# Nystrom attention and two MLPs on one core: another order of steps for the second MLP's weight sums, y loaded a group earlier, and low halves moved to GpSimd

## The chip, the core and the metric

The kernel runs on one core of a Trainium2 chip. The metric is the device time of one execution in microseconds (us). The engines are named as in the profile: PE (TensorE, matrix products), DVE (VectorE), ACT (ScalarE), POOL (GpSimd) and SP (the queue that issues the transfers). Each engine runs its own instructions in the order in which they were written, and waits on semaphores for the others.

## The reference, cut

```python
def _attn_ref(q, k, v):                # 4 batches, 8 heads, 576 x 64, 32 landmarks
    A, Bm, C = sm(q, k_lm), sm(q_lm, k_lm), sm(q_lm, k)      # softmaxes
    Z = Bm.T / (norm1(Bm) * norminf(Bm) + 1e-06)
    for _ in range(6):
        Z = 2 * Z - Z @ Bm @ Z
    return A @ Z @ C @ v
def _moe_ref(x, w_in, w_out):          # 2304 tokens, 512 -> 2048 -> 512
    h = x @ w_in
    return (h - np.tanh(h)) @ w_out
def _moe2_ref(x, w_in, w_out):         # the same sizes
    h = x @ w_in
    return (h * np.tanh(softplus(h))) @ w_out
```

The result is `_moe2_ref` of `_moe_ref` of the attention. Inputs and outputs are float32.

## The kernel before

**Splitting.** A float32 factor is kept as two parts: a high half, which ACT makes by a copy to fp32r, and a low half, the difference that DVE or POOL makes with a `tensor_tensor`. A product is then three matmuls: high by high, high by low, low by high.

**First MLP.** It runs in 128 slots (NS = 128), one for 288 tokens and 128 of the 2048 hidden columns. Slot `s` issues `h1(s)` (6 matmuls, L635 to L637), `y1(s - 3)` in two halves (12 matmuls, L708, L709, L712) and `vec(s)`, which makes the activation on ACT and DVE: `mk` (L665), `g = h * e` (L671), `th` (L672), then for the slot before `g = q * g` (L682) and `copy_predicated` (L686), and for the slot before that the split of `g` into `gg` (L99 on ACT, L100 for the low half). `E()` chooses the engine of `mk` and of the low half: POOL in slots 24 to 103, DVE elsewhere. Up to slot 115 a scheduler may move instructions; from slot 116 on the order is as written.

**Second MLP.** The 2304 tokens are cut into 3 units of 768 (u = 0, 1, 2), the hidden columns into 8 parts (j). That makes 24 groups, k = 8u + j. A group multiplies 2 by 2 blocks by Strassen's scheme in Winograd's form, with 7 products p = 0 to 6 (`product`, L783 to L785, 6 matmuls each) and sums of blocks on either side. Between the products stand the units of the last group's second matrix (`o2_units`, L841 to L843); in group 0 there are the last halves of `y1` in their place. `combine(k, p)` takes a product out of PSUM (L806 on DVE), and `mish` makes the activation (L796 and L797 on ACT, L799 on DVE). Two PSUM buffers hold the products, so product p + 2 can only begin when `combine` of p has read its buffer.

**The weights' sums.** While unit 0 runs, `w2_cycles` decodes the second MLP's weights and makes the sums `X` (L185) and their halves `W2c[j][q]` (tiles P: high L178, low L182), and stores them; later units load them again. One cycle has 7 steps, one to a product: cycle j + 1 runs beside group j. The order in which the products need the halves is given by

```python
WI = ((1, 2), (1, 1), (0, 1), (0, 3), (0, 2), (1, 0), (0, 0))
```

so product 0 reads `W[1][2]` and product 1 reads `W[1][1]`, which is written with `W[1][0]` by the pair of instructions of shape 128x2x256 (128x512 in the profile).

**The y sums.** `y_prep(u)` loads four blocks of y for a unit, makes the sums `s1`, `s2`, `a21 - ...` (L742), and the halves `yk` (high L751, low L752) of seven operands; the tiles `AT` hold the seventh. `Y[u + 1, p]` lies in the buffer of `Y[u, p]`, so it can be written only between product p of the last group of a unit and product p of the next one. `part` and `parts` lay the generators' steps beside the products: one step of `y_prep` and one of `w2_cycles` at a product.

Of the kernel before, what the change touches and what calls it, by code (L numbers as in the profile page):

```python
# [8 lines left out]
F32 = mybir.dt.float32  # L9
# [20 lines left out]
def kernel(  # L30
# [19 lines left out]
    NS = 32 * B  # L50
# [91 lines left out]
    def w2_cycles():  # L142
        raws, halves = {}, {}

        def has(x, j):
            return 0 <= j < NJ

        def fetch(x, j):
            if has(x, j):
                raws[x, j] = load_raw(ONE[x](j))  # L150

        def cast(x, j):
            if has(x, j):
# [12 lines left out]

        def o_hi(x, j):
            if has(x, j):
                w = W2o[2 * j + (x == "d")] = wo_p.tile([128, 2, 512], F32R, tag="w", name="w")
                A.activation(out=w[:, 0, :], in_=o32[x, j], func=ACTF.Copy)  # L170

        def o_lo(x, j):
            if has(x, j):
                w = W2o[2 * j + (x == "d")]
                V.tensor_tensor(out=w[:, 1, :], in0=o32.pop((x, j)), in1=f32(w[:, 0, :]), op=ALU.subtract)

        def hi(W, i, src):
            A.activation(out=W[:, i:i + src.shape[1], 0, :], in_=src, func=ACTF.Copy)  # L178

        def lo(W, i, src):  # L180
            n = src.shape[1]
            V.tensor_tensor(out=W[:, i:i + n, 1, :], in0=src, in1=f32(W[:, i:i + n, 0, :]), op=ALU.subtract)  # L182

        def minus(o, x, y):
            V.tensor_tensor(out=o, in0=x, in1=y, op=ALU.subtract)  # L185

        def keep(j):
            for q in range(2):
                n = 4 - q
                nc.sync.dma_start(out=w2s[j][q][:, 0:n, :], in_=f32(W2c[j][q][:, 0:n].rearrange("p n t c -> p n (t c)")))  # L190

        fetch("a", 0)
        fetch("b", 0)
        for j in range(NJ + 1):
            i = j < NJ

            cast("a", j)
            if j:
                lo(W2c[j - 1][1], 0, rows[j - 1][:, 0:2])
                keep(j - 1)  # L200
                yield 0
            o_join("c", j - 1)
            yield 0
            cast("d", j - 1)
            yield 1

            if i:
                X = rows[j] = p2["X"].tile([128, 6, 256], F32, tag="X", name="X")
                joined("a", j, X[:, 0:4:3, :])
                yield 0  # L210
                cast("b", j)
            o_hi("c", j - 1)
            o_join("d", j - 1)
            yield 1

            fetch("c", j)
            if i:
                joined("b", j, X[:, 1:3, :])
                yield 0
            o_hi("d", j - 1)  # L220
            o_lo("c", j - 1)
            yield 1

            fetch("a", j + 1)
            if i:
                minus(X[:, 4:6, :], X[:, 1:3, :], X[:, 0:2, :])
                yield 0
            o_lo("d", j - 1)
            yield 1

            fetch("d", j)
            if i:
                W = W2c[j] = [P_p.tile([128, 4, 2, 256], F32R, tag="P", name="P") for q in range(2)]
                hi(W[1], 2, X[:, 0:1])
                hi(W[0], 0, X[:, 2:6])
                minus(X[:, 1], X[:, 2], X[:, 4])
            yield 1

            fetch("b", j + 1)
            if i:  # L240
                lo(W[1], 2, X[:, 0:1])
                yield 0
                minus(X[:, 0], X[:, 1], X[:, 3])
            yield 1

            cast("c", j)
            if i:
                hi(W[1], 0, X[:, 0:2])
                lo(W[0], 0, X[:, 2:6])
            yield 1  # L250

    def w2c_load(j):
        W = W2c[j] = [P_p.tile([128, 4, 2, 256], F32R, tag="P", name="P") for q in range(2)]
        for q in range(2):
            n = 4 - q
            nc.sync.dma_start(out=f32(W[q][:, 0:n].rearrange("p n t c -> p n (t c)")), in_=w2s[j][q][:, 0:n, :])
# [383 lines left out]
    def vec(s):  # L640
# [3 lines left out]
        if NW + 2 <= s < NS + 2:  # L644
            with tc.high_priority(20):
                g2 = sv[s - 2][0]
                gg = t1_p.tile([128, 2, HS], F32R, tag="gg", name="gg")
                split(g2, gg[:, 0, :], gg[:, 1, :], E())
                sv[s - 2] = gg
        if s == NS:  # L650
            A.preload_act_table_set("mish")
# [74 lines left out]
    def y_prep(u):  # L726

        def load(kh, th):
            t = raw_f32()[:, 0:2 * C2].rearrange("p (a n) -> p a n", a=2)
            n0 = 0  # L730
            while n0 < C2:
                i, o = divmod((2 * u + th) * C2 + n0, HS)
                n = min(C2 - n0, HS - o)
                nc.sync.dma_start(out=t[:, :, n0:n0 + n], in_=ys[i][:, 2 * kh:2 * kh + 2, o:o + n])
                n0 += n
            return t

        a21, a22, a11, a12 = load(0, 1), load(1, 1), load(0, 0), load(1, 0)
        s1, s2 = [p2["yf"].tile([128, 2, C2], F32, tag="yf", name="yf") for _ in range(2)]

        def tt(eng, o, x, y, op=ALU.subtract):
            (G if u == 0 else eng).tensor_tensor(out=o, in0=x, in1=y, op=op)  # L742

        def halves(p, t):
            if p < 6:
                y = p2["yk"].tile([128, 2, 2, C2], F32R, tag="yk", name="yk")
                y = Y[u, p] = [y[:, a] for a in range(2)]
            else:
                y = Y[u, p] = [AT_p.tile([128, 2, C2], F32R, tag="AT", name="AT") for a in range(2)]
            for a in range(2):  # L750
                A.activation(out=y[a][:, 0, :], in_=t[:, a], func=ACTF.Copy)  # L751
                V.tensor_tensor(out=y[a][:, 1, :], in0=t[:, a], in1=f32(y[a][:, 0, :]), op=ALU.subtract)  # L752
                yield 0

        yield 1
        tt(G, s1, a21, a22, ALU.add)
        yield 1
        tt(V, s2, s1, a11)
        yield from halves(0, a11)
        yield 1  # L760
        yield from halves(1, s2)
        tt(G, a21, a11, a21)
        yield 1
        yield from halves(2, a12)
        tt(V, s2, a12, s2)
        yield 1
        yield from halves(3, a21)
        yield 1
        yield from halves(4, s1)
        yield 1  # L770
        yield from halves(5, a22)
        yield 1
        yield from halves(6, s2)
        yield 1
# [110 lines left out]
    def group(k, bg2):  # L885
        if k:
            units = o2_units(k - 1)
        for p in range(7):
            product(k, p)
            if k:  # L890
                for _ in range(UNITS[p]):
                    next(units)
                gens = []
            else:
                cur[0] = NS + p // 2
                if p < 2 * LAG:
# [78 lines left out]
    if True:  # L975
# [44 lines left out]
            n += 1  # L1020
        gens = {}
        early = [NS - x for x in (14, 12, 10, 7, 5, 3, 1)]
        yearly = [NS - 26] + [NS - 24 + i + i // 3 for i in range(8)]

        def bg(s):
            b, i = s // 32, s % 32
# [38 lines left out]
        def bg2(k, p):  # L1065
# [58 lines left out]
```

## Time and profile before

| what | value |
|---|---|
| runs, median (lowest to highest) | 847.68 us (847.6 to 850.5), 3 runs |
| the profiled execution, its own time | 846.66 us |
| its span on the core | 844.9 us |
| around the span | 1.76 us |
| mean granted TensorE clock | 0.979 |
| PE busy | 797.4 us (94%) |
| DVE busy | 595.0 us (70%) |
| ACT busy | 510.1 us (60%) |
| POOL busy | 196.9 us (23%) |

The shares are means over stages with different limits. In a timeline a row's bracket is the time for which the engine stood idle before that row, and whose event ended it. The spans of DVE's instructions overlap by almost 0.1 us where one follows another, so their pace is read from start to start.

### The profile page before, as it was taken

What the parts mean: (1) busy time and instruction counts of PE and PEld (TensorE: products, weight loads), DVE (VectorE), ACT (ScalarE), POOL (GpSimd) and SP (SyncE); (2) the same over time, 40 slices, a digit from 0 to 9 for tenths busy, and PEclk for the clock granted to TensorE, in tenths of its full rate; (3) what the DMA queues carried; (4) which work ended last, traced back from release to release, by engine and by line L of the source; (5) the groups of instructions that cost most, each with busy time, mean ns of one, the idle gap of its engine ahead of it and who ended that gap; (6) DMA issues with size and microseconds to landing.
All of it is one profiled execution on the core that took longest, in us unless ns stands there. A gap on an engine that the chain in (4) does not pass through costs nothing. (4 is left out here: it accounts for less than half of the span.)

```text
span 844.9 us, 14775 instructions
## 1 busy us (share of the span) xinstructions
PE 797.4 (94%) x5384; PEld 673.9 (80%) x5384; DVE 595.0 (70%) x1315; ACT 510.1 (60%) x1213; POOL 196.9 (23%) x218
## 2 busy tenths in 40 slices
PE   4799999999999999989998999988999999999996
PEld 1446688789888998878987878877889898889885
DVE  7679999998799867899987777775434355333332
ACT  4586787888678867878885666555323235322322
POOL 0010007775688657770000000020000010000000
PEclk9599999999999999999999999999999999999998
DMA  9999231513034001301437557754523543522401
GB/s 319 323 339 352 108 133 50 184 51 108 35 123 162 1 31 51 123 31 50 130 138 264 187 224 251 259 188 161 199 88 100 181 144 124 209 91 91 172 1 74
DMA packets 41512, 123.62 MB, mean 146 GB/s; under 512 B 5856, under 2 KB 14560, under 8 KB 38368
## 3 DMA queue, kind: packets, MB, share of 16 engines
q1 hardware_dynamic: 40288, 118.49, 39.8%
q0 software_dynamic: 1152, 4.19, 1.2%
q8 instruction: 42, 0.69, 0.4%
q14 instruction: 30, 0.25, 0.1%
HBM read 94.36 MB, written 28.31 MB: 145 GB/s over the span
## 5 line engine op out<-in xcount | busy, mean ns | idle before, releaser
L796 ACT ACTIVATE gg<-x 128x384 fp32r<-128x384 f32 x72 | 37.8, 525 | 171.4 <-DVE x L806 170.9
L708 PE MATMUL y<-gg,w 128*128 128x288 f32 x448 | 134.0, 313 | 2.0 <-ACT gg L99 1.0
L709 PE MATMUL y<-gg,w 128*128 128x288 f32 x448 | 125.9, 296 | 0.0
L783 PE MATMUL h<-yk,P 128*128 128x384 f32 x288 | 99.0, 344 | 13.2 <-ACT P L178 5.9
L708 PEld LDWEIGHTS y<-gg,w 128*128 128x128 f32 x448 | 84.4, 188 | 21.9 <-issue 12.6
L712 PE MATMUL y<-gg,w 128*128 128x288 f32 x448 | 96.8, 298 | 3.3 <-POOL gg L100 2.4
L785 PE MATMUL h<-yk,P 128*128 128x384 f32 x288 | 98.1, 341 | 1.4 <-DVE P L182 0.7
L784 PE MATMUL h<-yk,P 128*128 128x384 f32 x288 | 97.1, 337 | 0.0
L100 POOL TENSOR_TENSOR gg<-g,gg 128x288 fp32r<-128x288 f32 x80 | 70.1, 876 | 112.9 <-ACT gg L99 110.6
L709 PEld LDWEIGHTS y<-gg,w 128*128 128x128 f32 x448 | 84.7, 189 | 1.1
L799 DVE TENSOR_TENSOR gg<-x,gg 128x384 fp32r<-128x384 f32 x72 | 40.2, 558 | 61.2 <-ACT x L797 61.2
L806 DVE TENSOR_TENSOR x<-x,h 128x384 f32<-128x384 f32 x72 | 39.8, 553 | 60.7 <-PE h L785 60.4
L665 POOL TENSOR_SCALAR mk<-s 128x288 uint8<-128x288 f32 x80 | 77.4, 968 | 10.7 <-ACT s L659 4.3
L686 DVE COPY_PREDICATED g<-mk,th 128x288 f32<-128x288 uint8 x128 | 75.6, 591 | 4.6
L843 PE MATMUL y<-w,gg 128*128 128x512 f32 x192 | 76.3, 398 | 0.0
L842 PE MATMUL y<-w,gg 128*128 128x512 f32 x192 | 76.3, 397 | 0.0
L712 PEld LDWEIGHTS y<-gg,w 128*128 128x128 f32 x448 | 71.5, 188 | 5.3 <-POOL gg L100 4.1
L841 PE MATMUL y<-w,gg 128*128 128x512 f32 x192 | 75.7, 394 | 0.0
L783 PEld LDWEIGHTS h<-yk,P 128*128 128x128 f32 x288 | 54.5, 189 | 25.4 <-ACT P L178 8.9
L742 POOL TENSOR_TENSOR yf<-raw 128x768 f32<-128x768 f32 x3 | 6.3, 2104 | 283.3 <-ACT x L797 168.2
L671 DVE TENSOR_TENSOR g<-h,s 128x288 f32<-128x288 f32 x128 | 56.8, 444 | 18.9 <-ACT th L660 18.4
L675 ACT ACTIVATE q<-q,bias_c 128x288 f32<-128x288 f32 x128 | 68.5, 535 | 2.4
(167 smaller groups left out, 1958.2 us busy)
## 6 DMA issues: line engine op xcount, KB each, us to landing
P<-w2s SPq DMA_DIRECT2D x16, 1024.0 KB, 4.9
w<-w1s SPq DMA_DIRECT2D x24, 512.0 KB, 4.5
P<-w2s SPq DMA_DIRECT2D x16, 768.0 KB, 5.6
w2s<-P SPq DMA_DIRECT2D x8, 1024.0 KB, 3.9
raw<-in_w1i_dram SPq DMA_DIRECT2D x16, 511.8 KB, 6.1
raw<-in_w1o_dram SPq DMA_DIRECT2D x16, 511.8 KB, 6.9
raw<-in_w2i_dram SPq DMA_DIRECT2D x16, 511.8 KB, 5.7
raw<-in_w2o_dram SPq DMA_DIRECT2D x16, 511.8 KB, 6.0
```

The source lines that it names most:

```text
L100: eng.tensor_tensor(out=L, in0=src, in1=f32(H), op=ALU.subtract)
L665: eng.tensor_scalar(out=mk, in0=e, scalar1=FT, scalar2=None, op0=ALU.is_ge)
L686: V.copy_predicated(out=g0, mask=mk0, data=t0)
L708: mm(yps[d], w[:, 0, c], gg[:, 0, :], start=(f == 0), stop=False)
L709: mm(yps[d], w[:, 1, c], gg[:, 0, :], start=False, stop=False)
L712: mm(yps[d], w[:, 0, c], gg[:, 1, :], start=False, stop=(f == NF - 1))
L783: mm(t, w[:, i, 0, c], y[a][:, 0], start=(a == 0), stop=False)
L784: mm(t, w[:, i, 0, c], y[a][:, 1], start=False, stop=False)
L785: mm(t, w[:, i, 1, c], y[a][:, 0], start=False, stop=(a == 1))
L841: mm(q, gg[:, 0, cs], w[:, 0, :], start=first, stop=False)
L842: mm(q, gg[:, 0, cs], w[:, 1, :], start=False, stop=False)
L843: mm(q, gg[:, 1, cs], w[:, 0, :], start=False, stop=last)
```

## The change

It has three parts.

- **Weights.** In `w2_cycles` the halves of `W[1][2]` are made at steps 3 and 4 (before: 5 and 6), the two subtractions that make `X[1]` and `X[0]` both at step 5 (before: 5 and 6), and the high half of `W[1][0:2]` at step 6 (before: 7). Its low half stays at step 1 of the next cycle. The low halves of the second matrix move from steps 3 and 4 to 4 and 6. The two tiles of a cycle are taken in the other order.
- **y.** For u = 1 and 2 the steps begin in the group next to last, at product 1 (before: product 6). The two blocks a21 and a22 are loaded into a pool `yl` of their own. The sums s1, s2 and a21 are made on POOL, and the low half of the second part of operands 1, 3 and 4 too. For u = 0 the steps stand at other slots, and the seventh operand's halves come in group 0.
- **First MLP.** From slot 107 on (NS - 21) the low half of `gg` is made on POOL (`late()`), 23 instructions; `mk` stays on DVE.

```diff
+    def late():
+        return G if 24 <= cur[0] < NS - 24 or cur[0] >= NS - 21 else V
...
             fetch("c", j)
             if i:
+                W = W2c[j] = w2c_tiles()
+                hi(W[1], 2, X[:, 0:1])
                 joined("b", j, X[:, 1:3, :])
-                yield 0
             o_hi("d", j - 1)
-            o_lo("c", j - 1)
             yield 1
...
                 minus(X[:, 4:6, :], X[:, 1:3, :], X[:, 0:2, :])
                 yield 0
-            o_lo("d", j - 1)
+                lo(W[1], 2, X[:, 0:1])
+            o_lo("c", j - 1)
             yield 1
...
-                hi(W[1], 2, X[:, 0:1])
                 hi(W[0], 0, X[:, 2:6])
                 minus(X[:, 1], X[:, 2], X[:, 4])
+                yield 0
+                minus(X[:, 0], X[:, 1], X[:, 3])
             yield 1
...
-                lo(W[1], 2, X[:, 0:1])
-                yield 0
-                minus(X[:, 0], X[:, 1], X[:, 3])
+                hi(W[1], 0, X[:, 0:2])
+            o_lo("d", j - 1)
             yield 1
...
-                hi(W[1], 0, X[:, 0:2])
                 lo(W[0], 0, X[:, 2:6])
...
-                split(g2, gg[:, 0, :], gg[:, 1, :], E())
+                split(g2, gg[:, 0, :], gg[:, 1, :], late())
...
+            t = p2["yl"].tile([128, 2, C2], F32, tag="yl", name="yl") if u and th else raw_f32()[
+                :, 0:2 * C2].rearrange("p (a n) -> p a n", a=2)
...
+                eng = G if u and a and p in (1, 3, 4) else V
+                tt(eng, y[a][:, 1, :], t[:, a], f32(y[a][:, 0, :]))
...
-        tt(V, s2, s1, a11)
+        tt(G, s2, s1, a11)
...
-        yearly = [NS - 26] + [NS - 24 + i + i // 3 for i in range(8)]
+        yearly = [NS - x for x in (26, 25, 24, 23, 22, 20, 18, 16, 14, 12, 9)]
...
-            if j == NJ - 2 and p == 6 and u + 1 < NU:
+            if j == NJ - 2 and p == 1 and u + 1 < NU:
                 gens["y"] = vec_only(y_prep(u + 1))
...
+            if j == NJ - 2 and p in (1, 2, 4, 5, 6) or j == NJ - 1 and p or j == 0 and p == 0:
                 mix.append(gens["y"])
```

**DVE at the end of a group of unit 0.** These rows stand in DVE's queue between the products 4 of one group and 1 of the next; X and P are the weights' sums and halves, w and y the second matrix, x, u and gg the group's own values. Before:

```order
L799 TENSOR_TENSOR gg<-x,gg 128x384
L806 TENSOR_TENSOR x<-x,h 128x384
L182 TENSOR_TENSOR P<-X,P 128x256
L799 TENSOR_TENSOR gg<-x,gg 128x384
L185 TENSOR_TENSOR X<-X 128x256
L806 TENSOR_TENSOR u_6630<-u_6630,h 128x384
L182 TENSOR_TENSOR P<-X,P 128x4x256
L799 TENSOR_TENSOR gg<-u_6630,gg 128x384
L182 TENSOR_TENSOR P<-X,P 128x2x256
```

After (line 809 is the old 799, 816 the old 806, 185 the old 182, 188 the old 185 and 178 the old 175):

```order
L809 TENSOR_TENSOR gg<-x,gg 128x384
L188 TENSOR_TENSOR X<-X 128x256
L816 TENSOR_TENSOR x<-x,h 128x384
L178 TENSOR_TENSOR w<-y,w 128x512
L809 TENSOR_TENSOR gg<-x,gg 128x384
L816 TENSOR_TENSOR u_6633<-u_6633,h 128x384
L185 TENSOR_TENSOR P<-X,P 128x4x256
L809 TENSOR_TENSOR gg<-u_6633,gg 128x384
L185 TENSOR_TENSOR P<-X,P 128x2x256
```

The subtraction that makes X[0] now stands two rows earlier, before the product's row, and a low half of the second matrix stands where the low half of W[1][2] stood. On ACT the high half that the last row reads stands ahead of the group's last `mish` instead of behind it.

**DVE in group 7, the last of unit 0.** yk, yf and AT belong to `y_prep(1)`. Before, from the joins of the second matrix on:

```order
L158 SCALAR_TENSOR_TENSOR y<-raw,top_127 128x512
L742 TENSOR_TENSOR yf<-yf,raw 128x768
L752 TENSOR_TENSOR yk<-raw,yk 128x384 x2
L806 TENSOR_TENSOR x<-x,h 128x384
L175 TENSOR_TENSOR w<-y,w 128x512
L752 TENSOR_TENSOR yk<-yf,yk 128x384
L799 TENSOR_TENSOR gg<-x,gg 128x384
L752 TENSOR_TENSOR yk<-yf,yk 128x384
L806 TENSOR_TENSOR x<-u_7399,h 128x384
```

After (line 161 is the old 158; 745 holds every sum and low half of `y_prep`):

```order
L161 SCALAR_TENSOR_TENSOR y<-raw,top_127 128x512
L745 TENSOR_TENSOR yk<-raw,yk 128x384 x2
L816 TENSOR_TENSOR x<-x,h 128x384
L809 TENSOR_TENSOR gg<-x,gg 128x384
L745 TENSOR_TENSOR yk<-yf,yk 128x384
L816 TENSOR_TENSOR x<-u_7404,h 128x384
```

The sum of 768 columns and one low half are gone from the rows, and a low half of the second matrix comes behind the product's row.

**POOL at its end.** Before, its queue closes with the sums of `y_prep`:

```order
L665 TENSOR_SCALAR mk<-s 128x288
L742 TENSOR_TENSOR yf<-raw,yf 128x768
L742 TENSOR_TENSOR yf<-raw 128x768
L742 TENSOR_TENSOR raw<-raw 128x768
L742 TENSOR_TENSOR yf<-raw 128x768
L742 TENSOR_TENSOR raw<-raw 128x768
```

After (103 is the old 100, 670 the old 665):

```order
L670 TENSOR_SCALAR mk<-s 128x288
L745 TENSOR_TENSOR yf<-raw,yf 128x768
L103 TENSOR_TENSOR gg<-g,gg 128x288 x23
L745 TENSOR_TENSOR yf<-yl 128x768
L745 TENSOR_TENSOR yf<-yf,raw 128x768
L745 TENSOR_TENSOR yl<-raw,yl 128x768
L745 TENSOR_TENSOR yk<-yf,yk 128x384
L745 TENSOR_TENSOR yk<-yl,yk 128x384
```

It gains the 23 low halves of `gg`, and for either later unit one sum and three low halves.

## Rows read from the trace of the kernel before

**Rows 1.** Windows: stretch, time, busy us of each engine, clock, DMA share, GB/s.
```profile
380.62:431.19 50.57, 49.11 (x358) 47.36 (x357) 49.25 (x136) 43.41 (x115) 1.04 (x1) 1.00 0.23 75
...
437.66:441.07 3.41, 3.41 (x15) 3.41 (x14) 2.36 (x5) 2.21 (x4) 0.00 (x0) 0.50 1.00 324
...
505.46:522.29 16.83, 16.18 (x78) 13.95 (x79) 12.89 (x24) 10.26 (x19) 0.00 (x0) 1.00 0.63 234
556.00:578.89 22.89, 17.25 (x79) 13.66 (x79) 16.26 (x27) 9.62 (x21) 2.63 (x1) 1.00 0.78 275
625.92:641.59 15.67, 15.67 (x80) 14.07 (x79) 5.93 (x11) 4.58 (x9) 0.00 (x0) 1.00 0.33 113
```
**Rows 2.** Timeline of PE: product 1's first matmul in groups 0, 1, 2, 8, 15, 16.
```profile
435.25 0.42 PE L783 MATMUL h<-yk,P 128*128 128x384 f32 x1 [1.17 <-DVE th L672]
...
453.40 0.44 PE L783 MATMUL h<-yk,P 128*128 128x384 f32 x1 [2.64 <-ACT P L178]
...
471.79 0.44 PE L783 MATMUL h<-yk,P 128*128 128x384 f32 x1 [0.54 <-ACT P L178]
...
578.89 0.41 PE L783 MATMUL h<-yk,P 128*128 128x384 f32 x1 [0.89 <-DVE u L806]
...
688.57 0.34 PE L783 MATMUL h<-yk,P 128*128 128x384 f32 x1
...
705.78 0.41 PE L783 MATMUL h<-yk,P 128*128 128x384 f32 x1 [0.89 <-DVE u L806]
```
**Rows 3.** Timeline of DVE at the end of group 4.
```profile
518.61 0.56 DVE L799 TENSOR_TENSOR gg<-x,gg 128x384 fp32r<-128x384 f32 x1 [0.81 <-ACT x L797]
...
521.12 0.56 DVE L799 TENSOR_TENSOR gg<-u,gg 128x384 fp32r<-128x384 f32 x1
...
522.27 0.69 DVE L182 TENSOR_TENSOR P<-X,P 128x512 fp32r<-128x512 f32 x1 [0.59 <-ACT P L178]
```
**Rows 4.** Timeline of ACT at the same place.
```profile
520.00 0.53 ACT L796 ACTIVATE gg<-u 128x384 fp32r<-128x384 f32 x1 [1.43 <-DVE u L806]
...
521.62 0.61 ACT L178 ACTIVATE P<-X 128x512 fp32r<-128x512 f32 x1
```
**Rows 5.** Timeline of DVE in slot 126, one round from L671 to L671.
```profile
428.39 0.44 DVE L671 TENSOR_TENSOR g<-h,s 128x288 f32<-128x288 f32 x1
...
429.12 0.45 DVE L100 TENSOR_TENSOR gg<-g,gg 128x288 fp32r<-128x288 f32 x1
429.48 0.45 DVE L682 TENSOR_TENSOR g<-q,g 128x288 f32<-128x288 f32 x1
...
430.45 0.44 DVE L671 TENSOR_TENSOR g<-h,s 128x288 f32<-128x288 f32 x1
```
**Rows 6.** Groups of DVE by line, slots 34 to 101, while POOL makes the low halves.
```profile
L686 DVE COPY_PREDICATED g<-mk,th 128x288 f32<-128x288 uint8 x68 | 42.9, 631 | 4.0
L682 DVE TENSOR_TENSOR g<-q,g 128x288 f32<-128x288 f32 x68 | 33.6, 494 | 1.4 <-ACT q L675 0.5
```
**Rows 7.** The same groups from 400 to 430 us, POOL idle.
```profile
L682 DVE TENSOR_TENSOR g<-q,g 128x288 f32<-128x288 f32 x13 | 5.8, 446 | 0.0
...
L686 DVE COPY_PREDICATED g<-mk,th 128x288 f32<-128x288 uint8 x12 | 5.8, 482 | 0.0
```
**Rows 8.** Timeline of DVE, product 2 of group 7.
```profile
560.77 0.96 DVE L742 TENSOR_TENSOR yf<-yf,raw 128x768 f32<-128x768 f32 x1 [1.84 <-DMA raw<-ys]
561.64 2.68 DVE L752 TENSOR_TENSOR yk<-raw,yk 128x384 fp32r<-128x384 f32 x2
```
**Rows 9.** Timeline of POOL, 545 to 570 us.
```profile
549.87 2.25 POOL L742 TENSOR_TENSOR yf<-raw 128x768 f32<-128x768 f32 x1 [168.20 <-ACT x L797]
...
560.80 2.63 POOL L742 TENSOR_TENSOR raw<-raw 128x768 f32<-128x768 f32 x1 [8.69 <-DMA raw<-ys]
```
**Rows 10.** Timeline of DVE in the group before, under POOL's first sum.
```profile
551.04 1.37 DVE L182 TENSOR_TENSOR P<-X,P 128x256 fp32r<-128x256 f32 x1
```
**Rows 11.** Groups of POOL by line, the whole span.
```profile
L100 POOL TENSOR_TENSOR gg<-g,gg 128x288 fp32r<-128x288 f32 x80 | 70.1, 876 | 112.9 <-ACT gg L99 110.6 <-POOL c L571 0.7
```

More of the change, by code (lines that the diff above doesn't have):

```diff
@@ L232, in w2_cycles @@
             if i:
-                W = W2c[j] = [P_p.tile([128, 4, 2, 256], F32R, tag="P", name="P") for q in range(2)]
-                hi(W[1], 2, X[:, 0:1])
                 hi(W[0], 0, X[:, 2:6])
                 minus(X[:, 1], X[:, 2], X[:, 4])
+                yield 0
+                minus(X[:, 0], X[:, 1], X[:, 3])
             yield 1
@@ L247, in w2_cycles, with w2c_tiles @@
             if i:
-                hi(W[1], 0, X[:, 0:2])
                 lo(W[0], 0, X[:, 2:6])
             yield 1
+    def w2c_tiles():
+        return [P_p.tile([128, 4, 2, 256], F32R, tag="P", name="P") for q in range(2)][::-1]
     def w2c_load(j):
-        W = W2c[j] = [P_p.tile([128, 4, 2, 256], F32R, tag="P", name="P") for q in range(2)]
+        W = W2c[j] = w2c_tiles()
         for q in range(2):
@@ L728, in load @@
         def load(kh, th):
-            t = raw_f32()[:, 0:2 * C2].rearrange("p (a n) -> p a n", a=2)
+            t = p2["yl"].tile([128, 2, C2], F32, tag="yl", name="yl") if u and th else raw_f32()[
+                :, 0:2 * C2].rearrange("p (a n) -> p a n", a=2)
             n0 = 0
@@ L736, in load @@
             return t
-        a21, a22, a11, a12 = load(0, 1), load(1, 1), load(0, 0), load(1, 0)
-        s1, s2 = [p2["yf"].tile([128, 2, C2], F32, tag="yf", name="yf") for _ in range(2)]
         def tt(eng, o, x, y, op=ALU.subtract):
-            (G if u == 0 else eng).tensor_tensor(out=o, in0=x, in1=y, op=op)
+            eng.tensor_tensor(out=o, in0=x, in1=y, op=op)
         def halves(p, t):
@@ L751, in halves @@
                 A.activation(out=y[a][:, 0, :], in_=t[:, a], func=ACTF.Copy)
-                V.tensor_tensor(out=y[a][:, 1, :], in0=t[:, a], in1=f32(y[a][:, 0, :]), op=ALU.subtract)
                 yield 0
+                eng = G if u and a and p in (1, 3, 4) else V
+                tt(eng, y[a][:, 1, :], t[:, a], f32(y[a][:, 0, :]))
+        a21, a22 = load(0, 1), load(1, 1)
+        s1, s2 = [p2["yf"].tile([128, 2, C2], F32, tag="yf", name="yf") for _ in range(2)]
+        yield 1
+        a11, a12 = load(0, 0), load(1, 0)
         yield 1
@@ L757, in y_prep @@
         yield 1
-        tt(V, s2, s1, a11)
+        tt(G, s2, s1, a11)
+        yield 1
+        tt(G, a21, a11, a21)
+        yield 1
         yield from halves(0, a11)
@@ L761, in y_prep @@
         yield from halves(1, s2)
-        tt(G, a21, a11, a21)
         yield 1
         yield from halves(2, a12)
-        tt(V, s2, a12, s2)
+        tt(V if u else G, s2, a12, s2)
         yield 1
@@ L901, in group @@
                     p2["g3"] = ctx.enter_context(tc.tile_pool(name="g3", bufs=3))
+                    p2["yl"] = ctx.enter_context(tc.tile_pool(name="yl", bufs=2))
             mix = bg2(k, p)
@@ L1071, in bg2 @@
                 w2c_load((k + 1) % NJ)
-            if j == NJ - 2 and p == 6 and u + 1 < NU:
+            if j == NJ - 2 and p == 1 and u + 1 < NU:
                 gens["y"] = vec_only(y_prep(u + 1))
-                mix.append(gens["y"])
-            if j == NJ - 1 or j == 0 and p == 0:
+            if j == NJ - 2 and p in (1, 2, 4, 5, 6) or j == NJ - 1 and p or j == 0 and p == 0:
                 mix.append(gens["y"])
```

## The prediction

> **What bounds the kernel now.** I read the windows first, then the waits of PE as its timeline shows them, then DVE and ACT where PE waits. PE is the bound over most of the span: in a group of unit 1 it is busy for all of 15.67 us, while DVE is busy for 5.93 and ACT for 4.58 [rows 1]. That 15.67 us is the floor of a group. The change touches none of PE's work, so it can only give back idle time of PE, and the reader should look for that time. It lies in five places.
>
> First, slots 107 to 127, from 380.62 to 431.19 us. DVE is busy for 49.25 of 50.57 us and PE idle for 50.57 - 49.11 = 1.46 us [rows 1]. DVE is the slower one by a little.
>
> Second, groups 0 and 1. PE waits 1.17 us ahead of product 1 of group 0, for DVE's last reading of a first-MLP product, and 2.64 us ahead of product 1 of group 1, for a high half of the weights [rows 2]. After the first wait the granted clock is 0.50, which is 1.2 GHz, for 3.41 us [rows 1], and a second such stretch follows the second wait. At half clock 3.41 us do the work of 1.7.
>
> Third, groups 2 to 7. From 471.79 to 556.00 there are five groups [rows 1, 2], 84.21 / 5 = 16.84 us each, 1.17 above the floor. Each has one wait of about 0.54 us ahead of product 1 [rows 2]; the rest of the 1.17 is its third matmul, which waits for the low half, and the slow restart. The rows of DVE and ACT show why: the high half of W[1][0:2] (L178, 128x512) stands on ACT behind the group's last `mish` and ends at 522.23, and DVE has stood idle for 0.59 us when its low half begins at 522.27 [rows 3, 4].
>
> Fourth, group 7, whose period is 22.89 us [rows 1], 7.22 above the floor. DVE waits 1.84 us for the load of a11, makes a sum of 768 columns, and two low halves take 2.68 us where POOL works beside them [rows 8, 9]. The products are then read late, and PE waits for their PSUM buffers up to 578.89 [rows 2].
>
> Fifth, group 15: 705.78 - 688.57 = 17.21 us [rows 2], 1.54 above the floor.
>
> **The change, part by part.** Each term is worked out against the profiled execution, 846.66 us, span 844.9.
>
> *Low halves of `gg` on POOL.* One round of DVE is 430.45 - 428.39 = 2.06 us, of which L100 holds 429.48 - 429.12 = 0.36 [rows 5]. Without it the round is 1.70. What POOL costs DVE is read from slots in which POOL made the same low half: there L686 took 631 ns and L682 494, against 482 and 446 with POOL idle, which is 149 + 48 = 197 ns a slot [rows 6, 7]. So a round is about 1.90 us. The other work of DVE in the stretch is 50.57 - 20 x 2.06 = 9.4 us; the stretch would need 20 x 1.90 + 9.4 = 47.4 us, under the 49.11 that PE needs. PE then bounds it: **-1.5 us**. Bounds: nothing, if the 23 low halves, 876 ns each on POOL against 0.45 us on DVE [rows 5, 11], come late for `y1`; -3.0, if the restarts after PE's waits go too.
>
> *Groups 0 and 1.* DVE comes to group 0 earlier by four low halves less their hindrance, 4 x (0.36 - 0.20) = 0.6; the wait of 1.17 us goes; the idle 0.6 at the tail goes; and the first stretch at half clock, 1.7, need not come. Against it, the two low halves of AT now stand in group 0, 0.48 us each (0.36 x 384 / 288 by rows' starts) [rows 5]. That is 0.6 + 1.2 + 0.6 + 1.7 - 1.0 = 3.1. DVE and ACT hand each other the work here and are the bound, so I take **-3.0**. A wait ahead of product 1 of group 1 stays, since group 0 has less PE work than the others and the same work on DVE. Bounds -1.0 (the chain moves by DVE's own gain alone) and -6.0 (both stretches at half clock gone).
>
> *Ends of groups 1 to 6, six times.* With the high half ahead of the last `mish`, ACT can make it in its idle 1.43 us before 520.00 [rows 4]. DVE's low half then follows the L799 of 521.12 directly, at about 521.26, and ends at 521.94. Product 1 could start at 521.6 to 521.75 (522.29 less the idle 0.54, and up to 0.15 for the overlap of two matmuls' spans, an estimate), and its third matmul needs the low half some 0.35 later, at 522 (15.67 us for 78 matmuls are 0.2 each, the narrow ones less). So a tenth or two may remain of 1.17: **6 x -1.0 = -6.0**. The sum X[0] leaves the tail too, and a low half of the second matrix, 0.6 us (the 0.69 of its size less the overlap of 0.08), comes into the gap of 0.81 us that DVE waits there anyway [rows 3]: nothing, as long as that cover holds; if not, it costs its 0.6. Bounds -7.0 (all of it) and -3.0 (the low half is late by half a microsecond each time).
>
> *POOL's sums in group 6.* Three sums of 768 columns, 2.25 to 2.63 us each [rows 9], run about 7 us in the middle of group 6. Under such a sum the low half of 128x256 took 1.37 us [rows 10], where the one twice as wide takes 0.69 alone [rows 3]: about 1.0 us of waiting. Three sums can cost DVE 3.0 in that way. DVE is busy for 12.89 of 16.83 us there [rows 1], and the 3.9 us of idle time cover most of it: **+1.0**, bounds 0 and +3.0. The Trainium skill, page "SBUF — State Buffer", section "Who interferes with whom", speaks against this part: a DVE instruction with two SBUF inputs waits for the whole of a GpSimd instruction that reads SBUF. The trace agrees, since the 1.37 us end just after POOL's sum (552.41 and 552.12); by the rule at its worst three whole sums, 7.1 us, would block DVE, and less the 3.9 idle the term would be +3.2. The sums of unit 2 fall into group 14, where DVE is busy for 6 of 15.7 us: nothing.
>
> *Group 7.* The load is a group earlier, so 1.84 goes. DVE loses the sum (0.96), and three low halves (0.48 each, 1.4): of 16.26 us busy [rows 1] some 13.9 stay, and the 1.7 that POOL cost two low halves (2.68 against 2 x 0.48) goes in part. POOL's three low halves of 384 columns, 876 x 384 / 288 = 1170 ns each (an estimate from rows 11), hold back a low half or an `mish` by up to 0.8 us each. That fits into 15.67 with about 1 us lost at the end of the group, where DVE and ACT alternate: **-6.2**. Bounds -7.2 and -3.0.
>
> *Group 15.* The same without the weights' sums, 1.54 lost, nearly all from the same late load: **-1.4**, bounds -0.8 and -1.5.
>
> The pool `yl`, the other order of tiles and the later low halves of the second matrix cost nothing: those halves are read a group later, and the loads wait on nothing that is late. If the loads waited behind a store in SP's queue, group 7 would fall to its bound of -3.0.
>
> Sum: -1.5 - 3.0 - 6.0 + 1.0 - 6.2 - 1.4 = **-17.1 us**. 846.66 - 17.1 = 829.6. The median of the runs is 847.68, 1.02 above the profiled run, so I give **830.6 us**.
>
> **The rivals.** *Waits handed on.* The low half at product 1, and the readings of the products in group 7, are late by other work in DVE's queue, and PE's waits shrink to half. Ends of groups -3.0, group 7 -3.0 and groups 0 and 1 -1.5, with the rest as above: -1.5 - 1.5 - 3.0 + 1.0 - 3.0 - 1.4 = -9.4, so 838.3. For it: DVE and ACT alternate at the tail, and a wait in one shows in the other. Against it: at 521.12 DVE has no more than one row ahead of the low half.
>
> *More comes back.* The clock stays at 2.4 GHz through groups 0 and 1 and POOL hinders nothing: -3.0 - 6.0 - 7.0 + 0 - 7.2 - 1.5 = -24.7, so 823.0. Against it: group 0 is short on PE.
>
> *Slower: POOL takes over DVE.* If a low half on POOL held DVE not 0.2 but 1.4 us a slot (L682 and L686 each waiting for most of 876 ns), the stretch of the slots would need 20 x (1.70 + 1.40) + 9.4 = 71.4 us instead of 50.57, +20.8, and the sum would be 20.8 - 15.6 = +5.2: 852.9. It decides, against no change, from (50.57 + 15.6 - 9.4 - 34) / 20 = 1.14 us a slot on, and the measured hindrance is 0.2 [rows 6, 7].
>
> *It does not do what it says.* The scheduler keeps the old order in the slots and the tail waits for another row, so the time stays within half a per cent, 843 to 852. The order of the rows speaks against it.
>
> **How the numbers follow.** The forecast with its terms near their values, 824 to 836: 0.62. Waits handed on, 836 to 843: 0.18. More comes back, under 824: 0.12. No change: 0.04. POOL takes over: 0.04. The range 822 to 840 leaves out about 0.05 below and 0.14 above. Half a per cent, 4.2 us, is about what a measurement can tell from no change; faster 0.92, same 0.04, slower 0.04.
>
> **What would show it.** Right: PE's waits ahead of product 1 in groups 2 to 7 under 0.2 us and periods near 15.8; group 7 near 16.7 with no wait for `ys`; PE idle under 0.5 us in slots 107 to 127; L686 above 600 ns there. Wrong: periods that stay above 16.3; a new wait of `y1` for POOL's `gg`; product 1 of group 7 starting more than 2 us late behind POOL's sums; a granted clock of 0.50 in new places.

## The result and the profile after

| | before | after |
|---|---|---|
| median (lowest to highest) | 847.64 us (845.77 to 850.5) | 839.44 us (836.38 to 841.96) |
| ratio | | 0.9899 [0.9855, 0.9942] |
| profiled execution, its span | 846.66 us, 844.9 | 836.38 us, 834.6 |

The changed kernel is faster, by 8.2 us of the medians and 10.3 us of the profiled spans, where 17.1 were forecast. The profiled execution of after is the fastest of its runs; all terms below are taken from the two spans.

Windows of after, in the columns of [rows 1]: slots 107 to 127 up to product 0 of group 0; group 0; group 3; group 6; group 7 (each from product 1 to product 1).

```profile
380.70:436.40 55.70, 50.86 (x365) 48.38 (x364) 52.97 (x117) 45.00 (x118) 21.01 (x22) 1.00 0.19 68
438.57:454.24 15.67, 13.55 (x78) 12.43 (x79) 13.46 (x26) 12.27 (x24) 1.79 (x2) 1.00 0.73 257
487.57:503.49 15.92, 15.92 (x79) 14.03 (x78) 12.81 (x24) 10.26 (x19) 0.00 (x0) 1.00 0.67 248
535.29:552.06 16.77, 16.05 (x79) 13.86 (x78) 14.59 (x22) 8.57 (x16) 6.22 (x3) 1.00 0.79 266
552.06:570.13 18.07, 16.39 (x78) 13.86 (x79) 14.84 (x25) 11.12 (x24) 2.79 (x3) 1.00 0.77 278
```

Timeline of PE in after: product 1's matmuls, the answer to [rows 2], in groups 0, 1, 2, 7, 8, 15 and 16 (L793 is the first matmul, L795 the third, which needs the low half).

```profile
438.57 0.44 PE L793 MATMUL h<-yk,P 128*128 128x384 f32 x1 [0.18 <-DVE th L677]
...
440.17 0.44 PE L795 MATMUL h<-yk,P 128*128 128x384 f32 x1 [0.97 <-DVE P L185]
...
454.24 0.34 PE L793 MATMUL h<-yk,P 128*128 128x384 f32 x1
...
456.23 0.45 PE L795 MATMUL h<-yk,P 128*128 128x384 f32 x1 [1.47 <-DVE P L185]
...
471.64 0.34 PE L793 MATMUL h<-yk,P 128*128 128x384 f32 x1
...
552.06 0.41 PE L793 MATMUL h<-yk,P 128*128 128x384 f32 x1 [0.72 <-DVE u L816]
...
554.28 0.45 PE L795 MATMUL h<-yk,P 128*128 128x384 f32 x1 [1.63 <-DVE P L185]
...
570.13 0.41 PE L793 MATMUL h<-yk,P 128*128 128x384 f32 x1
...
679.83 0.34 PE L793 MATMUL h<-yk,P 128*128 128x384 f32 x1
...
695.49 0.34 PE L793 MATMUL h<-yk,P 128*128 128x384 f32 x1
```

Three things are to be seen. The groups got shorter: a middle group takes 15.92 us in place of 16.83 and group 15 695.49 - 679.83 = 15.66 in place of 17.21, both as expected; group 7 takes 18.07 in place of 22.89, where 16.7 was expected. The slots got longer: from slot 107 to product 1 of group 0 it is 438.57 - 380.70 = 57.87 us, where [rows 1, 2] give 435.25 - 380.62 = 54.63, although the wait ahead of that product fell from 1.17 to 0.18. And at product 1 of group 7 stand two new waits, 0.72 and 1.63 us.

The end of a group in after, DVE's timeline, the answer to [rows 3]:

```profile
518.66 0.56 DVE L809 TENSOR_TENSOR gg<-u,gg 128x384 fp32r<-128x384 f32 x1
519.14 0.69 DVE L185 TENSOR_TENSOR P<-X,P 128x512 fp32r<-128x512 f32 x1
```

The low half follows the last `mish` without a gap, as forecast.

In the slots, the longest wait of PE comes at 409.87. Timeline rows of SP, ACT, DVE and PE on the way to it:

```profile
404.84 0.69 DVE L161 SCALAR_TENSOR_TENSOR X<-raw,top 128x512 uint32<-128x512 uint32 x1
...
405.56 0.33 SPq L123 DMA_DIRECT2D raw<-in_w2o_dram  x1
406.06 0.33 SPq L123 DMA_DIRECT2D raw<-in_w2i_dram  x1
...
407.35 0.77 ACT L133 ACTIVATE top<-raw 128x512 f16<-128x512 bf16 x1 [1.28 <-DMA raw<-in_w2i_dram]
408.00 0.49 ACT L754 ACTIVATE yk<-yf 128x384 fp32r<-128x384 f32 x1
...
408.52 0.56 DVE L745 TENSOR_TENSOR yk<-yf,yk 128x384 fp32r<-128x384 f32 x1 [1.46 <-ACT yk L754]
...
409.87 0.40 PE L640 MATMUL h<-AT,P 128*128 128x288 f32 x1 [2.71 <-DVE th L677]
...
416.22 0.56 DVE L745 TENSOR_TENSOR yk<-raw,yk 128x384 fp32r<-128x384 f32 x1 [0.61 <-ACT yk L754]
...
417.07 0.55 DVE L745 TENSOR_TENSOR yk<-raw,yk 128x384 fp32r<-128x384 f32 x1
```

Read from the bottom: the last two low halves of y that read a `raw` buffer run at 416 and 417 us. In the kernel before they ran 20 us earlier:

```profile
395.74 0.54 DVE L752 TENSOR_TENSOR yk<-raw,yk 128x384 fp32r<-128x384 f32 x1
...
396.42 0.55 DVE L752 TENSOR_TENSOR yk<-raw,yk 128x384 fp32r<-128x384 f32 x1
```

Until then that buffer is not there for the weights. The load of 405.56 starts at the moment when L161 has read another one (404.84 + 0.69 = 405.53), the load of `w2i` stands behind it in SP's queue, and ACT waits 1.28 us for it. Behind ACT's waiting row stands a high half of y (408.00). DVE waits 1.46 us for that half, and behind DVE's waiting row stand the rows for which PE waits. So PE's wait may come from the load, which is late, or from the half of y, which stands in both queues behind the waiting row; yearly_early, below, tells the two apart.

### The profile page after: what moved, and what is told of

Its sections match the earlier page's. It is cut to its first block, busy times and chain, and to the rows that moved or that the text cites. A ratio compares the mean times of both kernels' runs of the same rounds, so it can differ in the third digit from the quotient of the medians.

```text
span 834.6 us, 14811 instructions
## 1 busy us (share of the span) xinstructions
PE 792.8 (95%) x5384; PEld 672.7 (81%) x5384; DVE 596.9 (72%) x1284; ACT 510.2 (61%) x1213; POOL 227.2 (27%) x249
## 4 chain that ended last, share of the span: by engine, by line
PE 73%; DVE 11%; ACT 6%; POOL 3%; issue 3%; DMA 3%; SPq 0%; ACTq 0%; DVEq 0%; POOLq 0%
PE h L795 7%; PE h L793 6%; PE h L794 6%; PE y L853 5%; PE y L852 5%; PE y L851 5%; PE y L713 5%; PE y L717 4%; PE y L714 4%; PE h L638 4%; PE m L330 4%; PE y L708 4%; PE m L852 3%; PE m L853 3%; PE m L851 3%
## 5 line engine op out<-in xcount | busy, mean ns | idle before, releaser
L103 POOL TENSOR_TENSOR gg<-g,gg 128x288 fp32r<-128x288 f32 x103 | 91.5, 888 | 155.1 <-ACT gg L102 152.7
L795 PE MATMUL h<-yk,P 128*128 128x384 f32 x288 | 97.5, 339 | 4.1 <-DVE P L185 4.1
L793 PE MATMUL h<-yk,P 128*128 128x384 f32 x288 | 97.4, 338 | 2.2 <-DVE u L816 1.2
L809 DVE TENSOR_TENSOR gg<-x,gg 128x384 fp32r<-128x384 f32 x72 | 44.2, 614 | 63.9 <-ACT x L807 63.2
L816 DVE TENSOR_TENSOR x<-x,h 128x384 f32<-128x384 f32 x72 | 39.8, 553 | 59.0 <-PE h L795 58.8
L691 DVE COPY_PREDICATED g<-mk,th 128x288 f32<-128x288 uint8 x128 | 76.1, 595 | 4.7
L687 DVE TENSOR_TENSOR g<-q,g 128x288 f32<-128x288 f32 x128 | 68.1, 532 | 1.4 <-ACT q L680 0.5
L664 ACT ACTIVATE s<-h 128x288 f32<-128x288 f32 x128 | 51.9, 406 | 24.9 <-PE h L642 13.6
```

The lines of the kernel that those rows point to most:

```text
L103: eng.tensor_tensor(out=L, in0=src, in1=f32(H), op=ALU.subtract)
L691: V.copy_predicated(out=g0, mask=mk0, data=t0)
L793: mm(t, w[:, i, 0, c], y[a][:, 0], start=(a == 0), stop=False)
L795: mm(t, w[:, i, 1, c], y[a][:, 0], start=False, stop=(a == 1))
```

## The experiments

The first four take the change apart: the weights' part alone, the y part for units 1 and 2 alone, the low halves of `gg` on POOL alone, and the changed kernel without the last.

```diff
w_only:  only the hunks of w2_cycles, w2c_tiles and w2c_load
y1_only: only the hunks of y_prep, yl and bg2; unit 0 keeps the old steps:
+    gens["y"] = vec_only(y_first(0))       # y_first: the y_prep of before
g_only:  only late() and its one call
no_g:    the changed kernel, with
-    split(g2, gg[:, 0, :], gg[:, 1, :], late())
+    split(g2, gg[:, 0, :], gg[:, 1, :], E())
```

> Only the weights' part: the new order of steps in w2_cycles and the other order of the two tiles, everything else as before. Both theories of the slots (held raw buffers by the late y halves, or POOL's low halves) expect group 0 to begin where it did before, near 432 us, give or take 0.5. Periods of groups 2 to 6 near 15.9 instead of 16.84, the wait for a high half (ACT, line 178 before) gone; groups 0 and 1 shorter by 3 to 5 us together; group 7 as long as before, near 22 to 23. Time about 839.5 us, 8 below the kernel before. If the weights' part gives nothing by itself, periods stay near 16.8 and the time near 847.

> Only the y part for units 1 and 2 (loads a group earlier, own buffers, sums and three low halves on POOL); unit 0's y, the weights and the slots as before. Group 0 begins near 432. Periods of groups 2 to 5 stay at 16.84; the one that ends with product 1 of group 7 grows to about 18, since POOL's three sums hold up DVE; group 7 near 18 (22.89 before), group 15 near 15.7 (17.21 before). Time about 842.5 us, 5 below. If POOL's sums take back all that the early load gives, the time stays near 847.

> Only the low halves of gg on POOL from slot 107 on; the rest as before. Theory 1 (the 4.4 us that the slots lost come from the y halves that stand later and hold the buffers into which the weights are loaded): group 0 begins at 430.5 to 432, time 845.5 to 847.5. Theory 2 (POOL's low halves hinder DVE more than they save): group 0 begins at 434 to 436, time 850 to 852.

> The changed kernel with the low halves of gg back on DVE from slot 107 on; the y and weights parts stay. Theory 1 (held buffers): group 0 begins no earlier than the 436.4 us of the changed kernel, 436 to 438, the wait of 2.7 us in slot 117 stays, time 838 to 842. Theory 2 (POOL's low halves): group 0 begins near 432 to 433, the wait is gone or under 1 us, time 833 to 836.

| kernel | median, us | ratio to before | slot 107 to product 0 of group 0 |
|---|---|---|---|
| w_only | 839.57 | 0.9895 [0.9865, 0.9925] | 51.1 |
| y1_only | 841.88 | 0.9921 [0.9894, 0.9948] | 51.4 |
| g_only | 850.62 | 1.004 [1.0024, 1.0057] | 54.0 |
| no_g | 840.82 | 0.9906 [0.9876, 0.9936] | 57.8 |

The weights' part alone is worth 7.6 us and the later units' y 5.3, against 847.18 for before in these runs, and both leave the slots at the 51.4 us of before (product 0 of group 0 begins there at 432.01, and 432.01 - 380.62 = 51.39). POOL's low halves alone make the kernel slower by 3.4 us. Without them the changed kernel still loses 6.4 us in the slots, and there its worst wait is longer, in PE's timeline of no_g:

```profile
413.60 0.61 PE L640 MATMUL h<-AT,P 128*128 128x288 f32 x1 [6.08 <-DVE th L677]
```

So two parts of the change lose time in the slots, each by itself. Why the late halves of y cost more without POOL's part is only partly followed. Two things are to be seen. The `yk` from a `raw` buffer that after makes at 390.43 comes at 400.76 in no_g, in slots whose order the scheduler makes:

```profile
400.76 0.57 DVE L745 TENSOR_TENSOR yk<-raw,yk 128x384 fp32r<-128x384 f32 x1
...
401.47 0.35 SPq L123 DMA_DIRECT2D raw<-in_w2i_dram  x1
```

The load of `w2i` starts when that row has ended (400.76 + 0.57 = 401.33), 10 us later than in after (391.12), and ACT then waits twice for `w2i`, 2.19 and 2.51 us. Here the held buffer does delay the loads. And the granted clock falls to 0.50, which is 1.2 GHz, at 411.6 us, when PE has stood idle since 407.5; it rises at 418.4. PE works from 413.60 on, so up to (418.4 - 413.6) / 2 = 2.4 of the 6.4 us can be the clock's (an estimate); after has no such stretch in its slots.

The next four ask whether the good parts add up, and undo one suspect at a time.

```diff
w_y1:         w_only and y1_only together
old_y0:       w_y1, and late() with its call
yearly_early: the changed kernel, with
-        yearly = [NS - x for x in (26, 25, 24, 23, 22, 20, 18, 16, 14, 12, 9)]
+        yearly = [NS - x for x in (26, 25, 24, 23, 22, 21, 20, 19, 18, 17, 16)]
sums_early:   the changed kernel, with
-            if j == NJ - 2 and p in (1, 2, 4, 5, 6) or ...
+            if j == NJ - 2 and p in (1, 2, 3, 4, 5) or ...
```

> The weights' part and the y part for units 1 and 2 together; unit 0's y and the slots as in the kernel before. Theory A (the changed kernel loses some 4 to 6 us in slots 107 to 127, because unit 0's later y steps hold the raw buffers that the weights' loads need and because the low halves of gg on POOL hold DVE back; the other parts add up): the two parts alone gave -7.6 and -5.3 us, so about -12.9, 834.3 us; product 0 of group 0 starts some 51.3 us after slot 107, no wait of TensorE over 1 us in the slots, group 7 near 18 us, the ends of groups near 15.9. Theory B (the parts stand in each other's way, whatever unit 0 does: the weights' steps and y's steps share DVE's idle time): no faster than the changed kernel, 838 to 841 us, with the slots still at 51.3 us and longer periods.

> The changed kernel with unit 0's y prepared as before, so the low halves of gg on POOL stay. Theory A (POOL's low halves hold DVE back more than they save it): the slots take 53 to 54 us against 51.3 without them, as with that part alone, and the time is 2.5 to 3.4 us above the kernel with the weights' part and the later units' y, 836.8 to 837.7 us. Theory B (POOL's halves pay once the weights' steps are in the new order): the slots take under 51 us and the time is at or below 834 us.

> The changed kernel, with the eleven steps of unit 0's y in eleven slots in a row, so that the last ends 16 slots ahead of the end of the first MLP and not 9. Theory A (the raw buffers, held by the late halves of y, make the weights' load and so ACT and DVE wait): the wait of 2.72 us near slot 116 goes, product 0 of group 0 starts 2 to 4 us earlier after slot 107 (52 to 54 us in place of 55.7), the time is 2 to 4 us below the changed kernel's, some 836 us. Theory B (it is POOL's low halves alone that make the slots longer): the slots still take 55 us or more and the time stays at 839.5 us.

> The changed kernel, with POOL's sums and the following steps of y one product of group 6 earlier (after products 1, 2, 3, 4, 5 in place of 1, 2, 4, 5, 6). Theory A (POOL's sums run into the end of group 6 and hold DVE's sum and low half there): the two waits of TensorE ahead of and in product 1 of group 7, 0.72 and 1.63 us, go, and the time is 1.5 to 2.5 us below the changed kernel's, some 837 us. Theory B (the end of group 6 is late because the weights' and y's steps are too much for DVE there, whenever POOL runs): the waits only move, within 0.5 us.

| kernel | median (lowest to highest), us | ratio to before | slots, as above |
|---|---|---|---|
| w_y1 | 833.52 (832.47 to 834.11) | 0.9831 [0.9813, 0.9849] | 51.14 |
| old_y0 | 838.16 (835.57 to 838.69) | 0.9877 [0.9852, 0.9902] | 53.83 |
| yearly_early | 837.90 (836.29 to 839.99) | 0.9885 [0.9861, 0.991] | 53.78 |
| sums_early | 839.00 (836.13 to 841.16) | 0.9895 [0.9867, 0.9922] | 55.2 |

w_y1: the parts add up (-7.6 and -5.3, and 847.44 - 833.52 = 13.9 measured), and it beats the changed kernel by 5.9 us. old_y0 shows the price of POOL's low halves once more: 4.6 us, 2.7 of them in the slots. Where those lie shows in the groups of DVE by line in the slots. First w_y1, then old_y0 (the same instructions, three lines further down):

```profile
L684 DVE TENSOR_TENSOR g<-q,g 128x288 f32<-128x288 f32 x20 | 10.0, 499 | 0.0
L688 DVE COPY_PREDICATED g<-mk,th 128x288 f32<-128x288 uint8 x20 | 9.8, 489 | 0.0
L100 DVE TENSOR_TENSOR gg<-g,gg 128x288 fp32r<-128x288 f32 x21 | 9.5, 452 | 0.3 <-ACT gg L99 0.2
...
L667 DVE TENSOR_SCALAR mk<-s 128x288 uint8<-128x288 f32 x20 | 6.1, 304 | 0.0
L754 DVE TENSOR_TENSOR yk<-raw,yk 128x384 fp32r<-128x384 f32 x6 | 3.3, 547 | 0.0
L185 DVE TENSOR_TENSOR X<-X 128x256 f32<-128x256 f32 (+1 forms) x3 | 1.6, 525 | 0.0
L158 DVE SCALAR_TENSOR_TENSOR X<-raw,top 128x512 uint32<-128x512 uint32 x2 | 1.4, 686 | 0.0
```

```profile
L687 DVE TENSOR_TENSOR g<-q,g 128x288 f32<-128x288 f32 x21 | 12.0, 571 | 0.0
L691 DVE COPY_PREDICATED g<-mk,th 128x288 f32<-128x288 uint8 x20 | 10.2, 512 | 0.1
L670 DVE TENSOR_SCALAR mk<-s 128x288 uint8<-128x288 f32 x20 | 10.0, 502 | 1.1 <-ACT s L664 1.1
...
L757 DVE TENSOR_TENSOR yk<-raw,yk 128x384 fp32r<-128x384 f32 x6 | 5.0, 830 | 0.0
L188 DVE TENSOR_TENSOR X<-X 128x256 f32<-128x256 f32 (+1 forms) x3 | 2.7, 910 | 0.0
...
L161 DVE SCALAR_TENSOR_TENSOR X<-raw,top 128x512 uint32<-128x512 uint32 x2 | 2.0, 998 | 0.1
```

L100 is gone from DVE, 9.5 us. Nearly all of it comes back: `mk` (502 - 304) x 20 = 4.0, the product of L687 72 x 20 = 1.4, L691 0.5, the halves of y 283 x 6 = 1.7, the sums `X` 385 x 3 = 1.2 and L161 0.6, 9.4 us in all, 0.47 a slot. By starts of rows the low half had taken only 0.36 a slot [rows 5], so the slots should be 20 x 0.11 = 2.2 us longer; they are 2.7.

yearly_early takes the wait of 2.71 us away, PE's longest wait in its slots is 0.45, and it brings the slots from 55.70 to 53.78, the value of old_y0. So the late halves of y cost what lies in between, 1.4 to 1.9 us (sums_early, which runs the same rows as the changed kernel, takes 55.2), and the cause is their lateness. But it is not the late load: `w2i` is loaded no earlier (25.8 us after slot 107 begins, 25.4 in after), and ACT waits for it as long as in after.

```profile
411.32 0.79 ACT L133 ACTIVATE top<-raw 128x512 f16<-128x512 bf16 x1 [1.34 <-DMA raw<-in_w2i_dram]
```

In old_y0 ACT waits 1.30 us there, and PE nowhere in the slots more than 0.46. What these two kernels lack is the half of y behind the waiting row. That a held buffer costs time is shown in no_g alone. In the medians (837.90 and 838.16 against 839.44) the step is near what the runs scatter.

sums_early told nothing of its question: every engine's queue in it reads row for row as in the changed kernel, since POOL has nothing else to do there, and so its sums begin when their loads have landed, wherever the code puts them. It is a second measurement of the changed kernel, 839.00 beside 839.44, with 2.25 us for the wait of 2.71.

That left the waits at product 1 of group 7. DVE's and POOL's timeline in after shows what stands there:

```profile
545.01 1.26 DVE L188 TENSOR_TENSOR X<-X 128x256 f32<-128x256 f32 x1
...
546.67 2.10 POOL L745 TENSOR_TENSOR yf<-yf,raw 128x768 f32<-128x768 f32 x1 [0.68 <-DMA raw<-ys]
...
547.00 0.54 DVE L816 TENSOR_TENSOR x<-x,h 128x384 f32<-128x384 f32 x1
547.46 1.86 DVE L178 TENSOR_TENSOR w<-y,w 128x512 fp32r<-128x512 f32 x1
...
548.73 2.30 POOL L745 TENSOR_TENSOR yl<-raw,yl 128x768 f32<-128x768 f32 x1
...
549.25 2.20 DVE L809 TENSOR_TENSOR gg<-x,gg 128x384 fp32r<-128x384 f32 x1
```

DVE's L178, 0.68 us at other places, ends 0.55 us behind POOL's second sum, and L809, else 0.56, ends 0.42 us behind the third, as if each had waited for the sum's end. Three kernels, all on top of w_y1, ask whether the lateness of the sums matters or that POOL makes them at all.

```diff
w_y1_load0: the loads of y, and all steps behind them, a product earlier
-            if j == NJ - 2 and p == 1 and u + 1 < NU:
+            if j == NJ - 2 and p == 0 and u + 1 < NU:
w_y1_dve:
-        tt(G, s2, s1, a11)
+        tt(V, s2, s1, a11)
-        tt(G, a21, a11, a21)
+        tt(V, a21, a11, a21)
w_y1_both:  both edits
```

> The kernel with the weights' part and the later units' y, with the loads of y issued one product of group 6 earlier (y's steps after products 0 to 4 in place of 1, 2, 4, 5, 6). Theory A (POOL's sums are late because their loads land late, and hold DVE at the end of group 6): POOL's sums begin some 2.3 us earlier, the two waits of 0.75 and 1.63 us at product 1 of group 7 shrink to under 0.5 in all, 1.5 to 2.5 us below 833.5, some 831.5 us. Theory B (whatever the time of the sums, DVE's own steps are late there; or the later loads wait for the raw buffers anyway): the waits stay and the time is within 0.7 us of 833.5.

> The kernel with the weights' part and the later units' y, with two of POOL's three sums (s2 and a21) on DVE, 0.96 us each. Theory A (POOL's sums hold DVE for longer than DVE would need to make them): the period of group 6 stays under 16.8 and the waits at product 1 of group 7 fall from 2.4 to under 1.2 us; 832 to 833 us. Theory B (the two sums and the low halves are too much for DVE at the end of group 6, POOL or not): the waits of 2.4 us stay or grow to 3.5; 833.5 to 835 us.

> Both edits, loads a product earlier and two of the three sums on DVE. Theory A: no wait over 0.5 us at product 1 of group 7, group 6 near 15.9 and group 7 near 16.5, 2 to 3 us below 833.5, some 831 us. Theory B: DVE's sums wait for the load of a11 with everything behind them, the waits stay and the time is 833 us or more.

w_y1_load0: 833.19 us, 0.9831 [0.981, 0.9851], no change. Counted from product 1 of group 6, POOL's first sum begins no earlier (at 9.0 us, 8.8 in w_y1) and the other two only 0.7 us earlier, without the gap that lay ahead of them. The wait moves with them: PE waits ahead of product 0 of group 7 instead of product 1. Neither theory had that. DVE and PE in its timeline:

```profile
542.12 2.19 DVE L856 TENSOR_TENSOR gg<-x,gg 128x384 fp32r<-128x384 f32 x1
544.24 2.03 DVE L185 TENSOR_TENSOR X<-X 128x256 f32<-128x256 f32 x1
...
546.88 0.66 PE L840 MATMUL h<-yk,P 128*128 128x384 f32 x1 [2.20 <-DVE x L863]
```

Behind that wait the granted clock is 0.50 for 3.41 us, from 546.65 on, where w_y1 has 1.00. So part of the time that group 7 takes there is the clock's, and what earlier sums would cost without it is not shown.

w_y1_dve: 831.46 us, 0.9812 [0.9791, 0.9834]. Two sums on DVE cost it 0.95 us each and nothing beside them is held:

```profile
543.27 0.68 DVE L175 TENSOR_TENSOR w<-y,w 128x512 fp32r<-128x512 f32 x1
543.88 0.95 DVE L792 TENSOR_TENSOR yf<-yf,raw 128x768 f32<-128x768 f32 x1
544.74 0.55 DVE L856 TENSOR_TENSOR gg<-x,gg 128x384 fp32r<-128x384 f32 x1
...
548.88 0.44 PE L842 MATMUL h<-yk,P 128*128 128x384 f32 x1 [1.32 <-DVE P L182]
```

Group 6 takes 15.91 us in place of 16.81 and the two waits of w_y1 (0.75 and 1.63) become one of 1.32. So the cause is that POOL makes the sums beside DVE; what is left is DVE's own work at the end of the group. The rows carry this reading more than the medians do, since the intervals of w_y1 and w_y1_dve overlap. w_y1_both: 833.69 us, 0.9841 [0.982, 0.9863]: there DVE's first sum waits 3.27 us for POOL's, with the whole queue behind it, and a stretch at 0.50 follows, from 545.6 to 549.0.

The last kernel moves the second of DVE's sums out of the end of group 6.

```diff
best: w_y1_dve, with
-        tt(V, a21, a11, a21)
-        yield 1
         yield from halves(0, a11)
+        tt(V, a21, a11, a21)
-            if j == NJ - 2 and p in (1, 2, 4, 5, 6) or ...
+            if j == NJ - 2 and p in (1, 2, 4, 5) or ...
```

> The kernel with the weights' part, the later units' y and s2 and a21 on DVE, in which the sum a21 is made behind the first low halves of y, at the start of group 7 and not at the end of group 6. Theory A (the 1.32 us that TensorE still waits in product 1 of group 7 are that sum, 0.94 us, ahead of the low half it waits for): the wait falls to about 0.4 us, the sum fits into group 7, and the time is 0.5 to 1.0 us under 831.5, some 830.7 us. Theory B (the wait is ACT's and DVE's turn-taking there, or group 7 has no room for the sum): the wait stays or comes back later in group 7, 831.5 us or more.

It takes 831.39 us, 0.9812 [0.979, 0.9834]. The wait falls from 1.32 to 0.56, but group 7 takes 17.53 us where w_y1_dve's takes 17.64: the sum fits only partly into group 7. The two kernels are equal, and both beat the kernel before and the changed one, by some 16 and 8 us.

## Why the prediction was half right

The time lies in the range, and the direction was right, but the gain was 10.3 us of span and not 17.1. By its terms, from the windows and rows shown:

| term | forecast | measured | from |
|---|---|---|---|
| slots, `gg` on POOL | -1.5 | +4.2 | 57.87 - 54.63 = 3.24, and 0.99 for the wait at product 1 |
| groups 0 and 1 | -3.0 | -3.5 | that wait 0.99; group 0 15.67 for 18.15 |
| six ends of groups | -6.0 | -5.6 | 0.99 at group 2 (471.64 - 454.24 for 18.39), 0.92 in the middle ones, taken for the sixth too |
| POOL's sums in group 6 | +1.0 | +2.5 | group 6 16.77 where 15.9 was open, and the 1.63 in product 1 |
| group 7 | -6.2 | -6.4 | 22.89 - 18.07, less that 1.63 |
| group 15 | -1.4 | -1.6 | 17.21 - 15.66 |

They add up to -10.4.

**Slots.** This term had the wrong sign, for two reasons. The hindrance of 197 ns a slot was taken from slots in which DVE made only L682 and L686 of what POOL can hold back [rows 6, 7]. In slots 107 to 127 DVE also makes `mk`, the halves of y and the weights' sums, and these were held too: 0.47 us a slot. Nor did the sign named for it come: L686, now L691, stayed at 512 ns. The price of a shared resource was measured where fewer instructions used it. The second reason is the lateness of unit 0's steps of y, which were spread to slots up to 9 ahead of the end: 1.4 to 1.9 us went there (7.3 us of median between w_y1 and no_g, where POOL does not hold DVE, the clock's part included). The prediction priced these steps by DVE's time alone. It did not ask behind which row each half would stand on ACT and DVE, which cost the changed kernel its 2.71 us of wait, nor until when a step holds its `raw` buffer. Its sentence that "the loads wait on nothing that is late" does not hold: in after a load waits until 417.62 us for a `yk`, and in no_g that costs time.

**POOL's sums.** The mechanism was named and its bound of +3.0 held. The 3.9 us of DVE's idle time did not cover it: the prediction had the sums in the middle of group 6, but they came at 544 to 551 us (the second waited for its load until 546.67), and the end of the group is the place where PE waits for DVE. Whether sums in the middle would have been covered is not shown; in w_y1_load0 they came only 0.7 us earlier, and the wait moved with them. By the rule that the prediction cites, of the section "Who interferes with whom" of the Trainium skill's page "SBUF — State Buffer", it had worked out +3.2 at the worst; the +2.5 lie nearer to that than to +1.0. The trace agrees with the rule in detail: L178 and L809, both with two inputs in SBUF, take 1.86 and 2.20 us, while L816, which reads PSUM, takes its usual 0.54 in the midst of them.

**The other terms** held within 0.6 us, the middle groups, group 7 and group 15 by their mechanism: the low half right behind the last `mish`, a11 there in time, group 15 without loss. Groups 0 and 1 came out near the forecast partly by luck. The prediction gave 1.7 of their gain to the clock, and no stretch at half clock came in them in after, where before has two of 3.41 us (the first in [rows 1], the second from 454.66 on). But yearly_early has one in group 0, from 442.6 us on, and takes 16.03 us for that group where after takes 15.67; best has one too and takes 15.79 where w_y1_load0, with the same rows there and no stretch, takes 15.50. So a stretch costs 0.3 to 0.4 in group 0. Instead, the 2.64 us ahead of product 1 of group 1 went, a wait that the prediction kept. A wait of 1.47 us now stands at the third matmul there, so the 0.99 at group 2 hold more than the end of a group: that wait, and the second stretch, which is gone.

**The rivals.** The time is that of "waits handed on" (838.3), but not by its way: at product 1 of groups 2 to 6 the waits that it kept are gone, and the loss is in the slots and under POOL's sums. "POOL takes over DVE" named the mechanism of the slots with 1.4 us a slot; 0.47 were measured, and the point from which the low halves no longer pay is 0.36 a slot, what DVE saves. "It does not do what it says" and "more comes back" fell.

## What to carry to other kernels

A bundle of edits can hide a loss inside its gain: here two parts won 13.9 us and two others gave 5.9 back, and only taking them apart showed it. Before work moves to an engine that hinders another, take the price from the stage where it will run, over every instruction of the hindered engine there. When a step is moved, look at what it will stand behind in each queue, and follow its buffers to the next one who wants them: a step behind a waiting row makes other engines wait too, and a late reader of a shared pool can delay the loads of quite other work.

## What the runs showed of the hardware

`mk`, a `tensor_scalar` with one input, went from 304 ns in w_y1 to 502 in old_y0 beside POOL's low halves, more than L687 (499 to 571) and L691 (489 to 512). The Trainium skill's page "SBUF — State Buffer", section "Who interferes with whom", says of trn2 that `tensor_scalar` can enter a mode that uses the port pair it shares with GpSimd; the trace agrees with that as far as `mk` is held, and does not show the mode. Which row pays depends on what stands beside POOL's: in after L687 took 685 ns and `mk` 413. DVE's rows that read PSUM were not held in any of these timelines (0.54 to 0.55 us). Stretches of 3.41 us at a granted clock of 0.50 came and went between the profiles of these kernels, near 155 us in eight of the fourteen and near 371 to 377 us in twelve. The prediction had named half clock in new places as a sign of being wrong. The stretch at 371.4 us in after, behind 1.93 us in which PE stood idle, is new against the profile of before, but it did not delay slot 107 (380.70, and 380.62 before).
